# Attention, dense layer and experts in one kernel: expert layer over token groups of 256, 1024, 1024 in place of 768, 768, 768

## The chip, the cores and the metric

One core of one Trainium2 chip runs one program. The metric is device time in microseconds (us): the median of the runs of one kernel on the core.

## The reference, cut to what is computed

```
p_packed = softmax(p k^T / 8) v ; a = softmax(q p_packed^T / 8) p_packed     # 4 batches, 8 heads, 576 positions, 32 packed
x = silu(a w_in) w_out                                                       # 2304 tokens, 512 -> 2048 -> 512
P = exp(x w_gate - max); 8 times: rows to 1, columns to 1, times 2304 / 8    # 2304 x 8 experts
out = sum over e of P[:, e] * (relu(x w1[e]) w2[e])                          # w1 512 x 1024, w2 1024 x 512
```

All 2304 tokens go through all 8 experts.

## The kernel before, in words

Each product of the dense layer and of the experts is made of three TensorE products: an operand is split into a high part (ScalarE copies it to fp32r, line 113) and a low part (VectorE subtracts, line 114), and high·high, high·low and low·high are added in PSUM. This pair, `split`, makes every "form" below. Every stationary operand is 128 x 128; the streamed one has as many columns as the matmul is wide.

**Front and dense layer.** The attention of the four batches and the first quarter (c = 0) of the dense layer's hidden columns run in an order that a planner (`Plan`, lines 150 to 205) writes out: tasks have an engine, a cost, a priority (the tables `P_A1` to `P_C1`) and buffers that they take and give; `LOADS` is the order of the loads on the DMA queue. The weights of the dense layer come as 64-bit words, which `conv` turns to fp32. When the attention is over, `close_att` frees its memory, and the conversions of the second quarter (c = 1) begin. Then c = 1, 2, 3 follow, each of 8 half batches: 4 tiles of `gemm1` (line 522, 6 matmuls of 288 columns, then silu and a split) and 4 tiles of `gemm2` (line 556, 12 matmuls of 288 columns, of the half batch before), and once per batch a product `u` (line 215). After each tile `pump()` lets one piece of background work be placed. At the end of c = 3 the background is `pre_forms`: the forms of x and of the first expert weights. Outside the planner's part the framework orders the instructions of each engine itself, by their place in the text and by when it expects buffers and operands.

**Experts.** The 2304 tokens are three groups of 768, in two halves of `BLK` = 384. A step is an expert and one half of its hidden columns: 16 steps in a group, 48 in all (`NS`). Up (`up`, line 849) is a Strassen-Winograd scheme: 7 products of 12 matmuls, each of 384 columns. Down of group 0 (`down`, line 892) is plain: 6 tiles of 12 matmuls of 512 columns. Down of groups 1 and 2 (`down7`, line 985) is again 7 products of 12 matmuls of 384 columns: `h_forms` makes 7 forms of the hidden values, 768 wide, from 4 differences; products are added to seven sums `M`, by a seeded bank and ScalarE's copies (lines 981, 993) or on VectorE (line 995).

The 7 forms of w1 and of w2 that each step needs are made in group 0 from the loaded weights (`w1_forms`, `w2_split`), stored in DRAM (`put`, line 650, 512 KB a form), and loaded (`get`) by groups 1 and 2. Group 0 has two buffers `T` for w2's forms and a ring of 16 buffers of 512 KB (`unit`) for the others. The column and row scaling of P (`sinkhorn`, lines 1005 to 1070) is a chain of small VectorE instructions that runs beside the first steps of group 0.

```
        for c in range(2):
            x = xf[g, p]
            for l, r in ((0, 0), (0, 1), (1, 0)):
                pe.matmul(ps, w[:, l, c, 128 * i:128 * i + 128], x[:, r, c],
...
        for f in range(4):
            w, h = w2t[s][f], hT[s, half, f]
            for l, r in ((0, 0), (0, 1), (1, 0)):
                pe.matmul(ps, h[:, l, 128 * tt:128 * tt + 128], w[:, r], start=(n == 0), stop=(n == 11))
```

Of the kernel before, what the change touches and what calls it, by code (L numbers as in the profile page):

```python
# [23 lines left out]
BLK = 384  # L24
FH = 512
EPS = 1e-9
CP = 6
# [3 lines left out]
P_A1 = [33.24, 7.01, 10.96, 13.54]  # L31
P_A2 = [49.27, 35.77, 44.16, 62.94]
P_U = [38.81, 12.22, 18.2, 4.05]
P_G1 = [23.84, 10.29, 0.56, 25.68]
P_G2 = [31.18, 0, 4.18, 31.19]
P_CI, P_CO, P_C1 = 0, 0.24, 33.0

LOADS = "k0 i2 i3 i1 i0 v0 q0 k1 q1 v1 o0 g k2 v2 o1 o3 q3 o2 v3 q2 k3"
# [35 lines left out]
def fused_kernel(  # L74
# [29 lines left out]
    a2b_p, a2b_st = pool("a2b", 1, side="right")  # L104
# [23 lines left out]
    class Plan:  # L128
# [13 lines left out]
        def order(self):  # L142
# [6 lines left out]
            while left:  # L149
# [46 lines left out]
                for c, k in t["give"]:  # L196
# [6 lines left out]
                 "a1T": 2, "ppm": 2, "ct": 4, "one": 1, "y": 4, "cr": 4})  # L203
# [49 lines left out]
    def plan_attention(b, early, late):  # L253
# [42 lines left out]
        for g in both:  # L296
# [8 lines left out]
            add(f"t{g}", "PE", 0.75, tr, [f"e{g}"], take=[("p", 2 - g)], give=[("a1", 1)])  # L305
# [22 lines left out]
        add("v", "PE", 1.3, pp, ["c0", "c1", ("v", b, 0), ("v", b, 1)], take=[("p", 1)],  # L328
# [287 lines left out]
    GRP = [(3, 4), (5, 0), (1, 2)]  # L616
    steps = [(g, e, fh) for g in range(3) for e in range(NE) for fh in range(2)]
    NS = len(steps)
    ORD = [1, 2, 6, 7, 5, 3, 4]
# [3 lines left out]
    st = {}  # L623
    raw1, raw2, wf, w2t, xf = {}, {}, {}, {}, {}
    x2d = tc.dram_tile([DM // 128, 128, NT], F32, name="x2d")

    def load_w1(s, kh):
        if s >= 2 * NE:
            return
# [6 lines left out]
    def load_w2(s, j):  # L636
        if s >= 2 * NE:
            return
        _, e, fh = steps[s]
        t = st["r2"].tile([128, 2, DM], F32, tag="r2", name=f"r2_{s}{j}")  # L640
# [4 lines left out]

    w1d, w2d = {}, {}

    def put(d, s, p, t):
        d[s, p] = tc.dram_tile([128, 2, 2, 256], F32, name=f"{'w1' if d is w1d else 'w2'}d{s}_{p}")
        nc.sync.dma_start(d[s, p], t.bitcast(F32))  # L650

    def get(d, s, p):
        t = unit([128, 2, 2, 256], F32R, f"{'w1' if d is w1d else 'w2'}l{s}_{p}")
        nc.sync.dma_start(t.bitcast(F32), d[s % (2 * NE), p])
        return t

    def w1_loads(s):
        for p in ORD:
            if s < NS:
                wf[s, p] = get(w1d, s, p)  # L660
            yield
            yield

    def w2_loads(s):
        for p in DORD:
            w2f[s, p] = get(w2d, s, p)
            yield
            yield

    def w1_forms(s, tmp):  # L670

        if s >= NS:
            return
        k1, k2 = raw1[s, 0], raw1[s, 1]
        a11, a21 = k1[:, :, 0:256], k1[:, :, 256:512]
        a12, a22 = k2[:, :, 0:256], k2[:, :, 256:512]

        def form(p, src):
            t = unit([128, 2, 2, 256], F32R, f"wf{s}_{p}")
            split(t[:, 0], t[:, 1], src)  # L680
            wf[s, p] = t
            put(w1d, s, p, t)

        form(1, a11)
        yield
        form(2, a12)
        yield
        s1, s2, s3, s4 = tmp(s, 1), None, None, None
        dve.tensor_tensor(s1, a21, a22, op=ALU.add)
        s2 = tmp(s, 2)  # L690
        dve.tensor_tensor(s2, s1, a11, op=ALU.subtract)
        form(6, s2)
        yield
        s3 = tmp(s, 3)
        dve.tensor_tensor(s3, a11, a21, op=ALU.subtract)
        load_w1(s + 1, 0)
# [4 lines left out]
        s4 = tmp(s, 4)  # L701
        dve.tensor_tensor(s4, a12, s2, op=ALU.subtract)
        form(3, s4)
        yield
        form(4, a22)
        load_w1(s + 1, 1)
        yield

    def w2_split(s):
        if s >= NS:  # L710
            return
        w2t[s] = []
        for j in range(2):
            for f in range(2):
                t = unit([128, 2, DM], F32R, f"w2t{s}{j}{f}")
                split(t[:, 0], t[:, 1], raw2[s, j][:, f])
                w2t[s].append(t)
                for p in ((1,) if j == 0 else (2, 4)):
                    if f == 0:
                        w2d[s, p] = tc.dram_tile([128, 2, 2, 256], F32, name=f"w2d{s}_{p}")  # L720
                    c = 256 if p == 4 else 0
                    nc.sync.dma_start(w2d[s, p][:, :, f], t[:, :, c:c + 256].bitcast(F32))
                yield

        k1, k2 = raw2[s, 0], raw2[s, 1]
        a11, a21 = k1[:, :, 0:256], k1[:, :, 256:512]
        a12, a22 = k2[:, :, 0:256], k2[:, :, 256:512]

        def form(p, src):
            t = st["T"].tile([128, 2, 2, 256], F32R, tag="T", name=f"T{s}_{p}")  # L730
            split(t[:, 0], t[:, 1], src)
            put(w2d, s, p, t)

        s1 = s_tmp(s, 11)
        dve.tensor_tensor(s1, a21, a22, op=ALU.add)
        s2 = s_tmp(s, 12)
        dve.tensor_tensor(s2, s1, a11, op=ALU.subtract)
        form(6, s2)
        yield
        s3 = s_tmp(s, 13)  # L740
        dve.tensor_tensor(s3, a11, a21, op=ALU.subtract)
        load_w2(s + 1, 0)
# [4 lines left out]
        s4 = s_tmp(s, 14)  # L747
        dve.tensor_tensor(s4, a12, s2, op=ALU.subtract)
# [322 lines left out]
    def nopump():  # L1071
        pass
# [213 lines left out]
```

## Time and profile before

| | us |
|---|---|
| median of 3 runs (1844.19 to 1844.93) | 1844.29 |
| the profiled execution, whole | 1845.25 |
| its span, first to last instruction | 1843.5 |
| TensorE busy in the span | 1812.1 |
| VectorE busy | 1317.4 |
| ScalarE busy | 924.9 |

The profile is one execution. PE is TensorE's matmuls, PEld its weight loads, DVE VectorE, ACT ScalarE, SP the queue that issues DMAs. Times in rows are us from the span's start, "x16" counts instructions, "out<-in" are tiles by their names in the program. Matmuls overlap in the array, so that the duration of one is longer than the distance to the next; the distance is read from rows that span many. VectorE's and ScalarE's durations overlap too, by about 0.1 us.

### The profile page before, as it was taken

The numbers are of one execution on the slowest core, as the hardware profiler recorded it, in microseconds if no ns is written. First come the engines' busy times: TensorE is split into PE (matmuls) and PEld (weight loads), VectorE is DVE, ScalarE is ACT, GpSimd is POOL, SyncE is SP. The second block draws the span as 40 slices with busy tenths as digits, with TensorE's granted clock in tenths as the row PEclk, the third lists the DMA queues.
The fourth block names the chain that finished last, engine by engine and source line by source line (L and its number), as shares of the span: only waits on it lengthen the run. The fifth ranks groups of instructions, "written<-read, shape, count | busy, mean of one in ns | idle before, by whom it ended". The sixth has DMA issues, their size and how long they took to land.

```text
span 1843.5 us, 29407 instructions
## 1 busy us (share of the span) xinstructions
PE 1812.1 (98%) x11127; PEld 1716.8 (93%) x11127; DVE 1317.4 (71%) x2228; ACT 924.9 (50%) x1816; POOL 1.0 (0%) x8
## 2 busy tenths in 40 slices
PE   6999999999999999999999999999999999999998
PEld 3898999998899989899999999999999999999998
DVE  6877644769987878787556667576786767666676
ACT  4876443545454545444254554454555445444544
POOL 0000000000000000000000000000000000000000
PEclk8999999999999999999999999999999999999999
DMA  9332100288898888888887878888888887888872
GB/s 336 117 92 93 58 13 1 75 285 319 304 338 297 312 296 306 302 308 296 302 263 250 261 258 261 261 245 266 259 275 287 250 266 256 263 247 261 262 251 95
DMA packets 169116, 437.18 MB, mean 237 GB/s; under 512 B 15360, under 2 KB 63632, under 8 KB 168976
## 3 DMA queue, kind: packets, MB, share of 16 engines
q1 hardware_dynamic: 168976, 435.31, 71.4%
q8 instruction: 88, 1.44, 0.3%
q14 instruction: 52, 0.43, 0.1%
HBM read 309.87 MB, written 125.38 MB: 236 GB/s over the span
## 4 chain that ended last, share of the span: by engine, by line
PE 95%; DMA 2%; DVE 1%; ACT 1%; issue 0%; SPq 0%; DVEq 0%; ACTq 0%
PE d L985 25%; PE X L849 22%; PE m L892 14%; PE Z L849 11%; PE g L556 10%; PE Y L849 5%; PE g L522 5%; PE u L215 1%; DMA k<-in_kT_dram 1%; DMA v<-in_v_dram 1%; PE s L215 1%; DMA rawin<-in_moe_w_in_dram 0%; PE lg L1011 0%; PE pp L323 0%; PE tp L302 0%
## 5 line engine op out<-in xcount | busy, mean ns | idle before, releaser
L985 PE MATMUL d<-hi,w2l 128*128 128x384 f32 x1792 | 495.0, 336 | 0.0
L114 DVE TENSOR_TENSOR lo<-hb,hi 128x768 fp32r<-128x768 f32 x224 | 214.2, 957 | 267.7 <-PE d L985 209.3
L985 PEld LDWEIGHTS d<-hi,w2l 128*128 128x128 f32 x1792 | 327.0, 188 | 6.8 <-ACT d L981 6.8
L985 PE MATMUL d<-lo,w2l 128*128 128x384 f32 x896 | 299.4, 334 | 0.0
L849 PE MATMUL X<-xf,w1l 128*128 128x384 f32 x1536 | 286.8, 334 | 0.0
L892 PE MATMUL m<-w2t,h 128*128 128x512 f32 x1152 | 280.4, 393 | 0.0
L849 PEld LDWEIGHTS X<-xf,w1l 128*128 128x128 f32 x1536 | 268.1, 188 | 0.1
L892 PEld LDWEIGHTS m<-w2t,h 128*128 128x128 f32 x1152 | 214.2, 188 | 41.9 <-DVE cp L860 0.3
L993 ACT COPY M<-d 128x384 f32<-128x384 f32 x232 | 111.6, 481 | 220.0 <-PE d L985 219.8
L113 ACT CAST hi<-hb 128x768 fp32r<-128x768 f32 x224 | 184.1, 836 | 57.7 <-DVE hb L946 30.9
L856 ACT COPY cp<-X 128x384 f32<-128x384 f32 x224 | 107.5, 480 | 209.8 <-PE X L849 209.8
L556 PE MATMUL g<-gT,woh 128*128 128x288 f32 x1024 | 206.4, 297 | 0.0
L556 PEld LDWEIGHTS g<-gT,woh 128*128 128x128 f32 x1024 | 163.8, 188 | 10.6 <-DVE gT L530 5.9
L985 PEld LDWEIGHTS d<-lo,w2l 128*128 128x128 f32 x896 | 168.2, 188 | 0.0
L556 PE MATMUL g<-gT,wol 128*128 128x288 f32 x512 | 150.7, 294 | 0.0
L849 PE MATMUL X<-xf,wf 128*128 128x384 f32 x768 | 146.7, 338 | 1.7 <-ACT cp L856 1.7
L849 PEld LDWEIGHTS X<-xf,wf 128*128 128x128 f32 x768 | 135.9, 188 | 8.3 <-ACT cp L856 2.9
L849 PE MATMUL Z<-xf,w1l 128*128 128x384 f32 x768 | 143.4, 334 | 0.0
L849 PEld LDWEIGHTS Z<-xf,w1l 128*128 128x128 f32 x768 | 134.0, 188 | 0.0
L995 DVE TENSOR_TENSOR M<-d,M 128x384 f32<-128x384 f32 x204 | 112.7, 552 | 10.9 <-PE d L985 10.6
L522 PE MATMUL g<-a2h,U 128*128 128x288 f32 x512 | 110.9, 301 | 5.8 <-ACT U L500 3.9
L981 ACT COPY d<-M 128x384 f32<-128x384 f32 x216 | 104.5, 484 | 18.1 <-DVE hb L822 14.8
(170 smaller groups left out, 2344.9 us busy)
## 6 DMA issues: line engine op xcount, KB each, us to landing
w1l<-w1d SPq DMA_DIRECT2D x224, 512.0 KB, 4.7
w2l<-w2d SPq DMA_DIRECT2D x224, 512.0 KB, 4.4
w1d<-wf SPq DMA_DIRECT2D x112, 512.0 KB, 5.3
r<-in_moe_w_dram SPq DMA_DIRECT2D x64, 512.0 KB, 5.9
w2d<-T SPq DMA_DIRECT2D x64, 512.0 KB, 4.3
w2d<-w2t SPq DMA_DIRECT2D x96, 256.0 KB, 3.6
rawin<-in_moe_w_in_dram SPq DMA_DIRECT2D x16, 512.0 KB, 4.8
rawout<-in_moe_w_out_dram SPq DMA_DIRECT2D x16, 512.0 KB, 4.7
```

The costliest lines, as they stand in the source:

```text
L113: act.copy(out=hi, in_=raw)
L114: eng.tensor_tensor(out=lo, in0=raw, in1=hi.bitcast(F32), op=ALU.subtract)
L215: pe.matmul(outs[i][32 * k:32 * k + 32, :n], lhsT[r, 32 * k:32 * k + 32], rhs(k)[r, cols], start=True, stop=True)
L522: pe.matmul(ps[:, :HS], lhs, rhs, start=(n == 0), stop=(n == 5))
L556: pe.matmul(ps[:, :HS], lhs, rhs, start=(n == 0), stop=(n == 3 * nf - 1))
L849: pe.matmul(ps, w[:, l, c, 128 * i:128 * i + 128], x[:, r, c], start=(n == 0 and p in ((1, 7) if g else (1, 2, 7))), stop=(n == 5), skip_g ...
L856: act.copy(out=t, in_=ps)
L892: pe.matmul(ps, h[:, l, 128 * tt:128 * tt + 128], w[:, r], start=(n == 0), stop=(n == 11))
L981: act.copy(out=ps, in_=m)
L985: pe.matmul(ps, w[:, l, c, 128 * d:128 * d + 128], r[:, c], start=(n == 0 and not seed), stop=(n == 5), skip_group_check=seed)
L993: act.copy(out=m, in_=ps)
L995: dve.tensor_tensor(m, ps, m, op=ALU.add)
```

## The change

- The expert groups become 256, 1024 and 1024 tokens. Group 0 (the first and the last 128 tokens) is plain on both sides: `up0` (4 blocks of 12 matmuls of 256 columns) and `down0` (2 tiles of 12 of 512). Groups 1 and 2 keep the 7 products, now 512 columns wide; hidden values, their forms and the sums `M` grow from 384 or 768 to 512 or 1024 elements.
- The forms of w1 for 12 of the 16 steps (`FRONT`) are made and stored by `pre_w1` during c = 1, 2, 3 of the dense layer, through two buffers `po`: 18, 28 and 38 forms are placed there in the text. Those of steps 5, 7, 9, 11 are made in group 0 (`w1_rest`). Group 0 itself needs only a plain split of w1 and w2 per step (`w1_split`, `w2_split`). w2's forms are made in group 1 (`w2_forms`), used there and stored; group 2 loads them.
- `pre0` splits x of group 0 and the weights of step 0 at the end of c = 3. The forms of x for group 1 are made in steps 10 to 14 of group 0, those for group 2 in group 1, stored and loaded in its last step.
- P is needed from expert 3 on (`LATE`); the results of experts 0 to 2 wait in six buffers.
- The planner's priorities, the order of the loads and two of its costs are others, and the conversions of c = 1 have three buffers in place of four.

```diff
-BLK = 384
+LG = 384
+NB = 512
+FRONT = [0, 1, 2, 3, 4, 6, 8, 10, 12, 13, 14, 15]
+RATE = {1: 18 / 64, 2: 28 / 64, 3: 38 / 44}
+LATE = 3
+AHEAD = 3
...
-LOADS = "k0 i2 i3 i1 i0 v0 q0 k1 q1 v1 o0 g k2 v2 o1 o3 q3 o2 v3 q2 k3"
+LOADS = "o2 i0 k0 i1 i3 v0 k3 i2 q0 o3 k1 g v3 k2 v1 q2 o1 v2 o0 q1 q3"
...
-                 "a1T": 2, "ppm": 2, "ct": 4, "one": 1, "y": 4, "cr": 4})
+                 "a1T": 2, "ppm": 2, "ct": 4, "one": 1, "y": 4, "cr": 3})
...
-            add(f"t{g}", "PE", 0.75, tr, [f"e{g}"], take=[("p", 2 - g)], give=[("a1", 1)])
+            add(f"t{g}", "PE", 0.9, tr, [f"e{g}"], take=[("p", 2 - g)], give=[("a1", 1)])
...
-        add("v", "PE", 1.3, pp, ["c0", "c1", ("v", b, 0), ("v", b, 1)], take=[("p", 1)],
+        add("v", "PE", 2.5, pp, ["c0", "c1", ("v", b, 0), ("v", b, 1)], take=[("p", 1)],
...
-    GRP = [(3, 4), (5, 0), (1, 2)]
+    TOK, TIL = {1: 1152, 2: 128}, {1: 9, 2: 1}
+    T0 = ((1, 8 * 128, 17), (0, 0, 0))
...
+    def pre_w1(todo, then):
+            def form(p, x):
+                t = st["po"].tile([128, 2, 2, 256], F32R, tag="po", name=f"po{s}_{p}")
+                split(t[:, 0], t[:, 1], x)
+                put(w1d, s, p, t)
...
+    def halves(name, s, j, raw):
+        h = unit([128, 2, 512], F32R, f"{name}h{s}{j}")
+        l = unit([128, 2, 512], F32R, f"{name}l{s}{j}")
+        split(h, l, raw)
...
+    def up0(s, j):
+        for i in range(2):
+            n = 0
+            f = slice(128 * (2 * j + i), 128 * (2 * j + i) + 128)
+            for k in range(4):
+                wh, wl = w1t[s][k // 2]
+                for w, x in ((wh, xs[0]), (wh, xs[1]), (wl, xs[0])):
+                    pe.matmul(ps[:, i], w[:, k % 2, f], x[:, k], start=(n == 0), stop=(n == 11))
...
+    def down0(s, tt):
+        for f in range(4):
+            wh, wl = w2t[s][f // 2]
+            h = h0[s, f // 2]
+            for l, w in ((0, wh), (0, wl), (1, wh)):
+                pe.matmul(ps, h[:, l, f % 2, 128 * tt:128 * tt + 128], w[:, f % 2],
+                          start=(fh == 0 and n == 0), stop=(fh == 1 and n == 11))
...
-    for name, n in (("cp", CP), ("T", 2), ("r2", 2), ("S", 3), ("h", 12), ("acc", 6)):
+    for name, n in (("xf", 7), ("cp", 5), ("xr", 2), ("pb", 2)):
...
-        for name, n, side in (("pb", 2, "left"), ("hb", 6, "left"), ("M", 8, "left"), ("hi", 5, "left"),
-                              ("lo", 4, "left")):
+    for name, n in (("hb", 6), ("hi", 3), ("lo", 3)):
...
+                if swap:
+                    nc.sync.dma_start(x_tile(2, p).bitcast(F32), xfd[p])
+                q = 7 * s + n + AHEAD
+                if q < 7 * NS:
+                    wf[q // 7, ORD[q % 7]] = get(w1d, q // 7, ORD[q % 7])
...
+            q = 7 * (s - 1) + n + AHEAD
+            if G0 <= q // 7 < 2 * G0:
+                next(forms)
+            elif 2 * G0 <= q // 7 < NS:
+                w2f[q // 7, DORD[q % 7]] = get(w2d, q // 7, DORD[q % 7])
```

## Rows read from the trace of the kernel before

**Rows 1.** The page: busy us, share of the span and count of each engine.
```profile
PE 1812.1 (98%) x11127; PEld 1716.8 (93%) x11127; DVE 1317.4 (71%) x2228; ACT 924.9 (50%) x1816; POOL 1.0 (0%) x8
```

**Rows 2.** Stretches: length; PE, PEld, DVE, ACT, POOL busy; granted clock, DMA share, GB/s.
```profile
0.00:20.00 20.00, 9.44 (x127) 5.21 (x127) 10.59 (x21) 9.52 (x20) 0.99 (x8) 1.00 0.95 339
20.00:40.00 20.00, 14.77 (x219) 6.79 (x219) 15.35 (x22) 8.61 (x18) 0.00 (x0) 0.77 0.99 317
40.00:60.00 20.00, 16.59 (x228) 11.64 (x229) 18.31 (x33) 17.89 (x41) 0.00 (x0) 0.89 0.83 279
...
100.00:141.30 41.30, 37.44 (x291) 36.37 (x289) 32.47 (x63) 33.18 (x76) 0.00 (x0) 0.99 0.34 103
141.30:222.60 81.30, 81.28 (x620) 77.27 (x621) 55.70 (x119) 44.69 (x103) 0.00 (x0) 0.97 0.25 80
222.60:303.60 81.00, 81.00 (x640) 76.98 (x639) 40.80 (x87) 33.99 (x82) 0.00 (x0) 1.00 0.04 13
303.60:386.90 83.30, 83.30 (x651) 80.13 (x652) 50.47 (x106) 35.73 (x88) 0.00 (x0) 1.00 0.29 105
386.90:480.00 93.10, 89.86 (x484) 77.36 (x485) 84.53 (x198) 46.15 (x90) 0.00 (x0) 1.00 0.86 304
480.00:500.00 20.00, 20.00 (x101) 17.96 (x100) 19.59 (x36) 9.91 (x19) 0.00 (x0) 1.00 0.84 301
480.00:896.40 416.40, 416.40 (x2073) 374.97 (x2072) 338.37 (x566) 195.10 (x376) 0.00 (x0) 1.00 0.87 308
896.40:1834.20 937.80, 937.80 (x5370) 929.86 (x5370) 632.10 (x965) 469.84 (x868) 0.00 (x0) 1.00 0.80 254
```

**Rows 3.** The chain of waits: start us, us, what; dense layer, group 0, group 2.
```profile
283.23 6.39 PE g L556 x48
...
638.49 2.76 PE m L892 x12
...
857.45 2.76 PE m L892 x12
...
1445.43 2.27 PE d L985 x12
...
1797.11 2.27 PE d L985 x12
```

**Rows 4.** Groups by line and form: instruction, tiles and count, then busy us, mean ns.
```profile
L404 DVE TENSOR_TENSOR a2l<-a2f,a2h 128x1152 fp32r<-128x1152 f32 x4 | 5.4, 1355 | 0.6 <-ACT a2h L399 0.6
L114 DVE TENSOR_TENSOR lo<-hb,hi 128x768 fp32r<-128x768 f32 x224 | 214.2, 957 | 267.7 <-PE d L985 209.3 <-ACT d L981 53.0 <-ACT hi L113 5.4
L114 DVE TENSOR_TENSOR wf<-S,wf 128x512 fp32r<-128x512 f32 x60 | 40.1, 685 | 0.3 <-ACT wf L113 0.2
L113 ACT CAST wf<-S 128x512 fp32r<-128x512 f32 x60 | 36.0, 621 | 17.7 <-DVE S L702 11.3 <-DVE S L691 3.8 <-DVE S L695 1.9
L914 DVE SCALAR_TENSOR_TENSOR acc<-m,P,acc 128x512 f32<-128x512 f32 x84 | 62.9, 749 | 34.2 <-PE m L892 34.1
...
L1048 DVE TENSOR_REDUCE csum<-P 128x8 f32<-128x144 f32 x8 | 3.3, 418 | 0.0
```

**Rows 5.** Group 0's stores of w2's forms, by tile.
```profile
DMA to landing us min/median/max: 2.6/4.3/8.5
```

**Rows 6.** DMA issues: KB each, median us to landing; 330 to 365 us, then 600 to 900.
```profile
w1d<-wf SPq DMA_DIRECT2D x3, 512.0 KB, 2.8
...
w1d<-wf SPq DMA_DIRECT2D x56, 512.0 KB, 5.4
```

**Rows 7.** By tile: dense weights of c = 2, 3: ns min/median/max, first and last start us.
```profile
L445 DVE CUSTOM_DVE_ANT_0 win<-rawin,ctin x8: 681/683/687, 151.8 to 216.9; 128x1024 uint16<-128x1024 uint16 x8
```

**Rows 8.** The chain of waits in the front: start us, us, what.
```profile
5.34 10.31 DMA v<-in_v_dram
...
26.93 9.11 DMA k<-in_kT_dram
...
135.34 3.85 DMA rawin<-in_moe_w_in_dram
```

More of the change, by code (lines that the diff above doesn't have):

```diff
@@ new lines, in pre_w1, with w1_split @@
+            s4 = sums(s, 4, ALU.subtract, a12, s2)
+            load_w1(nxt, 0)
+            load_w1(nxt, 1)
+            form(7, s3)
+            yield
+            form(5, s1)
+            yield
+            form(3, s4)
+            yield
+    w1t, w2t = {}, {}
+    def halves(name, s, j, raw):
+        h = unit([128, 2, 512], F32R, f"{name}h{s}{j}")
+        l = unit([128, 2, 512], F32R, f"{name}l{s}{j}")
+        split(h, l, raw)
+        return h, l
+    def w1_split(s):
+        w1t[s] = []
+        for j in range(2):
+            w1t[s].append(halves("w1", s, j, raw1[s, j]))
+            if s in FRONT and s + 1 < G0:
+                load_w1(s + 1, j)
+            yield
@@ new lines, in fused_kernel, with chain @@
+    open_("acc", 2 * LATE)
+    st["m"], s_ = pool("pm", 2, space=PSUM, side="left", reuse_waits="tile"); ctx.enter_context(s_)
+    def chain(*gens):
+        for g in gens:
+            yield from g
+    rest = iter(())
+    xg = x_forms(1, x_keep)
+    for s in range(G0 + 1):
+        wa = w1_split(s + 1) if s + 1 < G0 else iter(())
+        wb = w2_split(s) if 0 < s < G0 else iter(())
+        for slot in range(4):
+            if slot % 2 == 0:
+                if s < G0:
+                    up0(s, slot // 2)
+            elif s > 0:
+                if s == 2 * LATE + 2 and slot == 1:
+                    for _ in sk:
+                        pass
+                    load_pb(1, 0)
+                down0(s - 1, slot // 2)
+            if s == G0:
+                continue
+            next(wa if slot < 2 else wb, None)
+            if slot == 1 and s + 1 < G0 and s + 1 not in FRONT:
+                rest = w1_rest(s + 1)
+            if slot >= 1:
+                next(rest, None)
+            if s >= 1 and slot % 2:
+                next(sk, None)
+            if s >= 10 and slot:
+                next(xg, None)
+        for _ in rest:
+            pass
+        if s == G0 - 2:
+            for _ in xg:
+                pass
+        if s == G0 - 2:
+            for p in ORD[:AHEAD]:
+                wf[G0, p] = get(w1d, G0, p)
@@ L1205, in fused_kernel @@
+    for name in ("acc", "r2", "gh", "po"):
+        closers[name].close()
+    for name, n in (("hb", 6), ("hi", 3), ("lo", 3)):
+        open_(name, n, keep=True)
+    load_w2(G0, 0, "r1")
+    load_w2(G0, 1, "r1")
+    forms = chain(*(w2_forms(s) for s in range(G0, 2 * G0)))
+    xg = x_forms(2, x_store)
+    for s in range(G0, NS + 1):
+        swap = s + 1 < NS and steps[s + 1][0] != steps[s][0]
         hform = h_forms(s - 1) if s > G0 else iter(())
```

576 lines of the change are left out of this document (256 added, 320 removed).

## The prediction, made before the changed kernel ran

> **What bounds the kernel now.** I read the page's busy line first: TensorE is busy for 1812.1 of 1843.5 us [rows 1]. Then the stretches, to see where it is not [rows 2]: the front (to 141.3 us) leaves 23.1 us of TensorE idle (10.6, 5.2, 3.4 and 3.9 in the four rows that have any), the first 93.1 us of the expert layer leave 3.2 us, and the rest is full: 416.40 of 416.40 and 937.80 of 937.80 us. So from c = 1 on the time is the number of matmuls by the distance between them; another engine counts only where it makes TensorE wait. The chain of waits gives the distances, as periods that span many matmuls [rows 3]. A `gemm2` run of 48 matmuls of 288 columns takes 6.39 us: 133.1 ns each. In group 2, 12 steps of 168 matmuls of 384 columns lie between 1445.43 and 1797.11 us: 29.307 us a step, 174.4 ns each. In group 0, 7 steps lie between 638.49 and 857.45 us: 31.28 us a step; less 84 at 174.4 ns, 16.63 us are left for 72 of 512 columns: 230.9 ns each. From 288 to 384 columns that is 0.430 ns a column, from 384 to 512 it is 0.441.
>
> The terms below are differences against the span of that execution (1843.5 us; 1845.25 us whole, 0.96 above the median), and are put on the median of 1844.29 us. About 0.2% (3.7 us) is what a measurement here can tell from no change.
>
> **1. The matmuls: -16.7 us.** Before: 16 x 31.28 + 32 x 29.307 = 500.5 + 937.8 = 1438.3 us. After, groups 1 and 2 have the same 168 matmuls a step at 512 columns: 32 x 168 x 230.9 ns = 1241.3 us. Group 0 has 48 of 256 and 24 of 512 columns a step. No row has 256 columns; going on from 288 along 0.430 ns a column gives 119.3 ns, so 5.73 + 5.54 = 11.27 us a step, 180.3 us in 16. Sum 1421.6 us. There are 0.8% fewer columns and 1344 fewer matmuls of 7872. For 256 columns 133.1 ns (the 288 row) is the upper bound, if the weight loads set a floor there; that takes 10.6 us of the gain. Below, in proportion to columns, it is 118.3 ns. I take the line, since three widths lie on it.
>
> The Trainium skill's TensorE: Matmul & The Clock Gate, section Back-to-back issue gap, has columns / 2.4 GHz + 2.5 ns for one matmul after another. By it 384 columns would be 162.5 ns and 512 would be 215.8; the rows say 174.4 and 230.9, so the trace does not agree. The sum by the page would be 1340.6 to 1326.8, -13.8 us in place of -16.7, and the forecast 1838.
>
> **2. The dense layer: +3 us (0 to +8.5).** 84 forms of w1 come in, each a ScalarE cast of 0.621 and a VectorE subtraction of 0.685 us, with 48 sums of 0.685 us [rows 4]: VectorE +90.4 us. Out go the old forms at its end (14 of 0.55 us on halves of x with 8 differences, on the line of those rows, about 12 us, and 11 x 0.685), and in come 8 splits of 128 columns and 8 halves of 512 KB for step 0, about 8 us. The rows of c = 1, 2, 3 have 55.7 + 40.8 + 50.5 = 147 us of VectorE in 245.6; after, about 226, 92%. What hides it is VectorE's idle time. Rows on both sides of this: 19.59 of 20 us with TensorE at 20.00, and 84.53 of 93.1 (91%) with 3.24 us lost [rows 2]. At the second row's rate 245.6 us would lose 8.5. The first is steady work like this, the second a start with the sinkhorn beside it, so I take a third. ScalarE rises from 114 to about 160 of 245.6 us and is not near. Each engine takes its instructions in order: a cast that waits for one of the two `po` buffers holds up the silu behind it, and TensorE then waits for the PSUM bank that this silu frees. This is the rival below.
>
> The forms are placed late in the text (38 of 84 in c = 3, where 38 x 0.524 MB and 5.4 pairs of loads of 1.05 MB make 25.6 MB, over 44 of 64 pumps, 56 us: 457 GB/s, more than any row's 339). But work isn't kept to its place: the weights of c = 3, whose conversions stand in the text of c = 2 (from 222.6 us), were all done by 216.9 [rows 7]. So I expect the forms to spread from 141 us on, 65 MB with all loads in 245.6 us, 265 GB/s.
>
> **3. Group 0: +4 us (0 to +16).** The cover gets thin here, since TensorE's step shrinks from 31.28 to 11.27 us. VectorE per step: 4 halves of 1024 elements at 1.22 us (between 957 ns at 768 and 1355 at 1152 [rows 4]), 2 of 0.69 for the hidden values, about 0.7 for the sums (749 ns): 7.0 us. Steps 4, 6, 8, 10 add `w1_rest`: 4 sums and 4 splits, 5.5 us; steps 10 to 14 add 3.2 us for x's forms; the sinkhorn's 8 rounds have 8 small instructions of at most 418 ns, at most 27 us over steps 1 to 7. In all 112 + 22 + 15 + 27 = 176 us of 180.3 as the upper end, by durations that overlap. Each weight has buffers for two steps, so a step can lend to the next. Stalls at the rate of the like stretch before (3.24 in 93.1 us) are 6.3 us in place of 3.2, +3; I add 1 for the DMA, which has 58 MB in 180 us, 322 GB/s against 304 before, and 349 in steps 4 to 11 (2.1 MB of loads a step and 3.7 MB of stores in every second one). The upper end is each step's own surplus: 5.1, 5.1, 1.2 and 4.4 us in steps 4, 6, 8, 10, 15.8 us.
>
> **4. Groups 1 and 2: +2 us (0 to +10).** Step 38.79 us. VectorE in group 1: 11 of 1024 elements at 1.22, 30 of 512 at 0.69 (hidden values 8, additions 4 and 7, w2's forms 11), 1 for x: 35.1 us, 91% by durations; less about 0.08 us of overlap on each of 42, 31.7 us, 82%. Group 0 before had 338.37 of 416.40 (81%) and lost nothing [rows 2]. In group 2 it is 68%. The step before group 2 loads 7 x 1.05 MB of x beside 7.3 MB of weights, 379 GB/s: at most 4.5 us late at the fullest row's 339. With three buffers for `hi` and `lo` a late form shows sooner than with 5 and 4.
>
> **5. The front: -2 us (-10 to +9).** The work is the same; the order is not seen in this trace. Before, the chain waits 10.31 us for v and 9.11 for k, and 3.85 for raw weights that ScalarE's queue met too early [rows 8]. The bytes up to the end of v0 are the same in the new order (o2 i0 k0 i1 i3 v0 against k0 i2 i3 i1 i0 v0), the second k comes before a q fills the buffers, and the last loads are q1 and q3, for which half of the attention is already done, in place of k3. Against it: k0 is two loads (3 us at 339 GB/s) later, and c = 1 has three conversion buffers for four. The gain ends well inside the 23.1 us idle; the loss end is one more wait like the 9.11 row. I take little, on the side of the loads.
>
> **6. The tail: +0.5 us.** Last additions and stores are a third wider, with nothing beside them.
>
> Sum: -16.7 + 3 + 4 + 2 - 2 + 0.5 = -9.2; 1844.3 - 9.2 = **1835 us**.
>
> **Rivals.**
> - The front takes the 9 us wait for k away and more: 1844.3 - 16.7 - 10 + 9.5 = 1827 or less. For: VectorE has 14 us idle in the first 40 [rows 2]. Against: VectorE is already at 18.31 of 20 us from 40 on. Chance 0.20.
> - The gain is eaten: weight loads floor the 256 columns (+10.6), or stalls of 3 to 5 near half of their upper ends: 1841 to 1848. For: nothing here is narrower than 288. Against: 288 columns still lie on the line of 384 and 512. Chance 0.10.
> - Slower: VectorE sets the pace wherever the forms now lie. Upper ends of 2, 3 and 4 together, 8.5 + 15.8 + 10 = 34.3 us: 1844.3 - 16.7 - 2 + 0.5 + 34.3 = 1860. It decides from 18.2 us of stalls on. For: 91% with losses in the row from 386.9 us. Against: 98% without any in the row from 480. Chance 0.13.
> - Slower: the two `po` buffers pace the 84 forms. A buffer turns in 0.62 + 0.69 + the store + about 0.3 us of hand-overs; at a store of 5.4 us (the median at 304 GB/s) that is 3.5 us a form, 294 us in 245.6: +48, 1881. At 2.8 us (the median when little else ran) it is 2.2 us a form, 185 us [rows 6]. It decides from 4.2 us on; group 0's two `T` buffers had 4.3 in the middle [rows 5]. Against: with two stores out at a time and 265 GB/s the queue is shorter, and TensorE stood still for none of those. Chance 0.07.
> - The forecast, 1828 to 1840: 0.50.
>
> **How the numbers follow.** Faster 0.20 + 0.50 = 0.70, within 0.2% 0.10, slower 0.20. The range goes from 1822 (front at -10, stalls at half) to 1856 (most of the VectorE rival); outside lie some 0.06 below and 0.12 above.
>
> **What would show it.** Right: steps of 38.8 us in groups 1 and 2 and of 11.3 in group 0, 256-column matmuls at 119 ns, c = 1 beginning within a few us of 141 and taking 81.3 us a quarter, TensorE idle under 10 us behind it. Wrong: ScalarE waiting on the stores of `po` with silus behind it; TensorE waiting on VectorE in steps 4 to 10 of group 0; w1's forms unfinished at the end of c = 3; a front longer than 146 us.

## The result and the profile after

The changed kernel takes 1820.82 us (median of 4 runs, 1817.46 to 1822.23) against 1844.61 us of the kernel before beside it (1844.19 to 1845.57): a ratio of 0.9866, interval 0.9851 to 0.9882. The gain of 23.8 us is two and a half times the 9.2 forecast, and 1820.82 lies 1.2 us below the range of 1822 to 1856. The profiled execution took 1820.67 us, its span is 1818.7.

The busy line of the page, which answers to [rows 1]:

```profile
PE 1779.1 (98%) x9783; PEld 1513.0 (83%) x9783; DVE 1396.1 (77%) x1994; ACT 1004.6 (55%) x1674; POOL 1.0 (0%) x8
```

Stretches of the kernel after, with the columns of [rows 2]: the quarters c = 1, 2, 3, group 0 in two parts, groups 1 and 2, and then four slices of 20 us out of c = 1 and 2.

```profile
138.60:222.70 84.10, 80.09 (x593) 74.39 (x594) 71.79 (x147) 51.76 (x117) 0.00 (x0) 0.94 0.67 232
222.70:309.40 86.70, 84.58 (x642) 78.30 (x641) 70.46 (x141) 50.58 (x115) 0.00 (x0) 0.98 0.70 253
309.40:396.90 87.50, 87.50 (x676) 83.59 (x678) 63.52 (x125) 48.93 (x109) 0.00 (x0) 1.00 0.76 275
396.90:490.00 93.10, 93.04 (x626) 81.64 (x627) 85.20 (x162) 54.05 (x75) 0.00 (x0) 1.00 0.78 258
490.00:592.30 102.30, 98.91 (x604) 89.48 (x603) 64.53 (x76) 44.39 (x56) 0.00 (x0) 0.97 0.86 286
592.30:1204.00 611.70, 611.08 (x2694) 505.16 (x2694) 510.60 (x664) 356.55 (x553) 0.00 (x0) 1.00 0.74 248
...
140.00:160.00 20.00, 20.00 (x148) 19.00 (x148) 17.49 (x36) 13.64 (x34) 0.00 (x0) 0.92 0.61 212
...
180.00:200.00 20.00, 15.99 (x105) 13.50 (x104) 17.41 (x38) 11.11 (x26) 0.00 (x0) 0.83 0.64 215
...
220.00:240.00 20.00, 17.88 (x134) 15.68 (x132) 16.63 (x37) 11.88 (x27) 0.00 (x0) 0.97 0.81 280
240.00:260.00 20.00, 20.00 (x148) 19.39 (x142) 17.00 (x33) 11.94 (x27) 0.00 (x0) 0.95 0.64 237
```

The chain of waits of the kernel after, with the columns of [rows 3]: first the dense layer, then group 0, the start of group 1, and the same product 11 steps apart in group 2.

```profile
181.01 7.38 DMA rawin<-in_moe_w_in_dram
188.47 0.67 ACT ctin L438
...
190.64 0.61 ACT po L118
191.25 0.32 ACT graw L531
191.62 2.73 PE u L220 x16
...
440.69 2.75 PE d L883 x12
443.43 2.87 PE u L864 x24
...
559.17 14.00 DMA r<-in_moe_w_dram
...
592.28 2.72 PE X L1011 x12
...
1339.20 2.72 PE d L968 x12
...
1758.08 2.72 PE d L968 x12
```

Set against the boundaries of the kernel before (c = 1 from 141.3, the logits after c = 3 from 386.8, the first expert product at 392.1, group 0's last at 900.9, which is its end at 903.2 less 2.3 us for 13 matmuls of group 1 that ran ahead of it, the end at 1843.5), each term has a measured size:

| step | forecast | measured | from |
|---|---|---|---|
| 1 matmuls | -16.7 | -39.9 | 38.080 us a step in groups 1 and 2 ((1758.08 - 1339.20) / 11), 11.24 in group 0 (twice 2.87 and 2.75) |
| 2 dense layer | +3 | +12.8 | 258.3 us for 245.5 |
| 3 group 0 | +4 | +2.0 | 10.3 us over its matmuls for 8.3 |
| 4, 6 groups 1, 2, tail | +2.5 | +3.1 | 7.8 us over their matmuls for 4.7 |
| 5 front | -2 | -2.8 | c = 1 from 138.5 for 141.3 |
| sum | -9.2 | -24.8 | the spans differ by 24.8 |

So two terms were wrong, with opposite signs: step 1 by 23.2 us, step 2 by 9.8. They hide each other in part: with step 2 as forecast the time would have been about 1811 us. The experiments are on these two.

### The profile page after: what moved, and what is told of

Same layout as the page of the kernel before. It is cut to its first block, busy times and chain, and to the rows that moved or that the text cites. A ratio compares the mean times of both kernels' runs of the same rounds, so it can differ in the third digit from the quotient of the medians.

```text
span 1818.7 us, 26101 instructions
## 1 busy us (share of the span) xinstructions
PE 1779.1 (98%) x9783; PEld 1513.0 (83%) x9783; DVE 1396.1 (77%) x1994; ACT 1004.6 (55%) x1674; POOL 1.0 (0%) x8
## 4 chain that ended last, share of the span: by engine, by line
PE 82%; DMA 8%; DVE 6%; ACT 2%; issue 1%; SPq 0%; DVEq 0%; ACTq 0%
PE d L968 31%; PE X L1011 18%; PE Z L1011 9%; PE g L561 8%; PE Y L1011 5%; PE g L527 4%; DMA r<-in_moe_w_dram 4%; PE u L864 2%; PE d L883 2%; DMA rawin<-in_moe_w_in_dram 1%; DMA rawout<-in_moe_w_out_dram 1%; PE u L220 1%; DMA w1d<-po 1%; DMA k<-in_kT_dram 1%; DVE S L671 1%
## 5 line engine op out<-in xcount | busy, mean ns | idle before, releaser
L1011 PE MATMUL X<-xf,w1l 128*128 128x512 f32 x1536 | 368.8, 389 | 0.0
L1011 PEld LDWEIGHTS X<-xf,w1l 128*128 128x128 f32 x1536 | 288.3, 188 | 59.9
L119 DVE TENSOR_TENSOR lo<-hb,hi 128x1024 fp32r<-128x1024 f32 x224 | 273.4, 1221 | 51.6 <-ACT hi L118 50.6
L118 ACT CAST hi<-hb 128x1024 fp32r<-128x1024 f32 x224 | 236.0, 1054 | 107.8 <-PE d L968 99.8
L968 PE MATMUL d<-hi,w2f 128*128 128x512 f32 x896 | 294.6, 389 | 0.6 <-ACT d L964 0.6
L968 PE MATMUL d<-hi,w2l 128*128 128x512 f32 x896 | 293.1, 389 | 0.0
L968 PEld LDWEIGHTS d<-hi,w2f 128*128 128x128 f32 x896 | 168.2, 188 | 36.6 <-ACT d L964 1.7
L968 PEld LDWEIGHTS d<-hi,w2l 128*128 128x128 f32 x896 | 168.1, 188 | 35.2 <-ACT d L964 0.4
L1011 PE MATMUL Z<-xf,w1l 128*128 128x512 f32 x768 | 184.5, 389 | 0.0
L968 PE MATMUL d<-lo,w2f 128*128 128x512 f32 x448 | 174.3, 389 | 0.0
L968 PE MATMUL d<-lo,w2l 128*128 128x512 f32 x448 | 174.3, 389 | 0.0
L968 PEld LDWEIGHTS d<-lo,w2l 128*128 128x128 f32 x448 | 84.1, 188 | 17.5
```

The source lines that it names most:

```text
L118: act.copy(out=hi, in_=raw)
L119: eng.tensor_tensor(out=lo, in0=raw, in1=hi.bitcast(F32), op=ALU.subtract)
L968: pe.matmul(ps, w[:, l, c, 128 * d:128 * d + 128], r[:, c], start=(n == 0 and not seed), stop=(n == 5), skip_group_check=seed)
```

## Experiments

"Quarters" are the times of c = 1, 2, 3, from the first `gemm1` matmul of one to that of the next. Before they are 77.6, 81.3 and 86.6 us, after 84.1, 86.7 and 87.5. Each run has its own median of before beside it; between sets of runs those medians go from 1844.6 to 1846.7. Times without an interval are of one execution.

### What a matmul of 512 columns costs

**The kernel before, with the six down tiles of group 0 in a row** at the end of a step, in place of one behind each up product:

```diff
-            elif n > 0 and s > 0:
-                down(s - 1, n - 1)
-                pump_sk()
-                bg()
+            elif n == 6 and s > 0:
+                for d in range(6):
+                    down(s - 1, d)
+                    pump_sk()
+                    bg()
```

> The kernel before with one change: in the steps of group 0 the six plain down tiles follow each other after all seven up products, 72 matmuls of 512 columns in a row in place of six runs of 12 between products of 384 columns. Nothing is left out. Theory (mixed widths): matmuls of one width follow each other at columns / 2.4 GHz + 13.3 ns (384: 173.3, 512: 226.7 ns), and some ten matmuls after each change of width are a few ns slower; then the 72 take 16.36 us in each step, as the one such run in the trace before does, the step falls from 31.28 to 30.95 us, and the time by 5 us, to 1839. Rival (plain down): a tile with hidden values as its stationary operand costs 230.9 ns a matmul wherever it stands; then the step stays at 31.28 us and the time at 1844.

The chain of waits of this kernel in group 0:

```profile
629.07 16.36 PE m L892 x72
645.43 2.10 PE X L849 x12
647.54 2.08 PE Y L849 x12
...
876.64 5.48 PE m L892 x24
```

TensorE's largest wait between 380 and 480 us (line waited, releaser, us, times, longest):

```profile
PE cs L1051 <- DVE csum L1048: 10.0, 3, 5.7
```

72 matmuls of 512 columns in a row take 16.36 us, 227.2 ns each, and the step is (876.64 - 629.07) / 8 = 30.946 us in place of 31.28. The forecast of the whole time failed: 1856.87 us, ratio 1.0059 [1.0042, 1.0075]. The steps gained 0.33 us each, but the first ones lost more, since without a down tile to run in between TensorE waited 10.0 us for the column sums of the sinkhorn, and the granted clock from 387 to 480 us was 0.89, for 1.00 before [rows 2]. The price is settled all the same: 230.9 ns is the price of a 512-column matmul that stands in twelves between twelves of 384, and 227 that of one among its like. The trace of the kernel before had the same thing in its last step of group 0, where nothing of 384 columns stands in between, in a row of the chain that I had not used; with the last step's neighbours:

```profile
881.79 2.76 PE m L892 x12
884.55 2.10 PE X L849 x12
...
886.83 16.36 PE m L892 x72
903.19 1.93 PE Y L849 x11
905.12 2.08 PE X L849 x12
```

Twelve take 2.76 us after a change of width and 2.72 after their like (the chain after); of 384 columns twelve take 2.10 after a change and 2.08 without. Groups 1 and 2 of the changed kernel have one width throughout.

### Which part of the forms costs the dense layer 13 us

**No forms in the dense layer** (those of step 0 alone are made, and groups 1 and 2 load these for all the steps of `FRONT`):

```diff
+        k = 0 if d is w1d and s % G0 in FRONT else s % G0
-        nc.sync.dma_start(t.bitcast(F32), d[s % G0, p])
+        nc.sync.dma_start(t.bitcast(F32), d[k, p])
-    pre = pre_w1(FRONT, 0)
+    pre = pre_w1([0], 0)
```

> The kernel after without the background forms of w1: only those of step 0 are made and stored; groups 1 and 2 load step 0's forms for the other eleven steps, so that the loads there stay the same. Left out: 77 casts, 77 subtractions, 44 sums, 77 stores and 22 loads of the dense layer. If the forms are the cause of the longer dense layer, c = 1 to c = 3 return from 258.3 us to 245.5, as before, and the time to about 1808. If the cause is the three buffers or the other order, they stay above 252.

1810.13 us; quarters 77.5, 81.3 and 86.6, which are the kernel before's. So the forms are the whole loss, and the third conversion buffer or the other priorities have no part in it by themselves. **A fourth conversion buffer**, as before (`pool("cv", 3` to `4`), says the same from the other side:

> The kernel after with four buffers in place of three for the raw dense weights and their conversions (the planner's order of the front stays as it is). Nothing is left out. Theory (late weights): c = 1 and c = 2 are 6 us longer each than before because conversions of dense weights stand in ScalarE's queue ahead of silus and wait for loads that land late beside the stores of w1's forms. If the three buffers are what makes these loads start late, c = 1 to c = 3 (258.3 us from the first gemm1 of c = 1 to the logits) fall by 6 us or more, to 252, and the time to 1814. Rival (traffic): the loads are late because of the forms' stores and loads beside them; then a fourth buffer gives under 2 us.

1818.10 us, ratio 0.9850 [0.9835, 0.9864]; quarters 79.0, 87.7, 90.3, 257.0 in all.

Four runs then took one part of the forms away each. **The forms made, but only step 0's stored** (`if s == 0: put(w1d, s, p, t)`, and the same `k` for the loads):

> The kernel after with all forms of w1 made in the dense layer, but only those of step 0 stored (groups 1 and 2 load step 0's forms for the other eleven). Left out: 77 stores of 512 KB. VectorE and ScalarE do the same work. Theory (late weights): the DMA traffic is what makes the weights late and the two po buffers slow, so c = 1 to c = 3 fall to within 3 us of 245.5. Rival (VectorE or ScalarE full): they stay above 254, since both engines have as much to do as in the kernel after.

**Raw weights loaded and stored, no arithmetic** (in `form`, for all steps but 0, a store of the raw tile in place of the split, and no sums):

> The kernel after with the stores and loads of w1's forms in the dense layer, but without their making: for eleven of the twelve steps the raw weights are stored in the form's place. Left out: 77 casts, 77 subtractions and 44 sums. Theory (engines): with the stores gone but the forms made, c = 1 to c = 3 still took 256.8 us, so the casts, subtractions and sums in the queues of ScalarE and VectorE are the cause, and here they fall to 245.5 to 248 us. Rival (traffic): stores and loads delay the dense weights by themselves; then they stay above 252.

**All forms made and stored, from step 0's raw weights** (22 loads left out):

```diff
-            load_w1(nxt, 0)
-            load_w1(nxt, 1)
+            if nxt == then:
+                load_w1(nxt, 0)
+                load_w1(nxt, 1)
+            else:
+                raw1[nxt, 0], raw1[nxt, 1] = raw1[s, 0], raw1[s, 1]
```

> The kernel after with all forms made and stored, but from step 0's raw weights each time: 22 loads of 512 KB of the dense layer are left out (the forms are then those of step 0 under eleven other names). Theory (VectorE full): casts, subtractions, sums and stores are as many as before, so c = 1 to c = 3 stay above 255. Rival (waits in order for these loads): they fall to 250 or less.

**The 48 sums on GpSimd** (`nc.gpsimd.tensor_tensor` in `sums`, for `pre_w1` alone):

> The kernel after with the 48 sums of the forms in the dense layer made by GpSimd in place of VectorE. Nothing is left out. Theory (VectorE full): in the run without stores VectorE was 18.8 of 20 us busy from 140 to 300 us, so 29 us less of VectorE's work there give back half or more of the 12.8 us: c = 1 to c = 3 at 252 or less, the time at 1814. Rival (waits in order): the time is lost where a cast or a sum waits in its queue for a load and holds up what is behind; then c = 1 to c = 3 stay within 3 us of 258.

| | quarters | sum | time |
|---|---|---|---|
| no stores | 81.3, 88.9, 86.6 | 256.8 | 1819.67 |
| loads and stores alone | 78.0, 88.7, 86.6 | 253.3 | 1815.54 |
| no loads | 77.9, 83.9, 86.6 | 248.4 | 1811.61 |
| sums on GpSimd | 90.3, 86.7, 91.8 | 268.8 | 1833.81, ratio 0.9939 [0.9924, 0.9954] |

The stretches of c = 1 and 2 without the loads:

```profile
137.50:215.50 78.00, 76.82 (x590) 71.25 (x591) 71.90 (x150) 53.27 (x120) 0.00 (x0) 1.00 0.58 210
215.50:299.40 83.90, 83.24 (x642) 77.70 (x641) 72.31 (x146) 51.36 (x115) 0.00 (x0) 1.00 0.57 218
```

VectorE is busy here for 71.90 of 78.00 and 72.31 of 83.90 us, 89% of both together, more than the 83% of the changed kernel's two (142.25 of 170.8): the same work in less time, and TensorE stands idle for 1.8 us. So VectorE's share is not what costs. Part of this run's small loss is luck, though. The granted clock of its c = 1 is 1.00, while the kernel before has 0.97 there [rows 2], after a wait of 3.9 us before its first `gemm1`. That is some 2.4 us of the 245.5 (0.03 of 81.3), so that from an equal start the loss without loads is about 5 us and not 2.9.

Traffic alone, with VectorE at the level of before, costs 7.8 us, in a single wait of 4.5 us and the lower clock behind it (0.96 in c = 2). Without the stores 11.3 of the 12.8 us stay. What the three runs take away (9.9, 5.0 and 1.5 us) is more than the whole, so the parts don't add, and no one of them accounts for the loss alone.

The sums on GpSimd met neither expectation. On GpSimd a sum takes 1331 to 1535 ns, and VectorE's own subtractions get longer beside it, from 684 to 799 ns in the mean:

```profile
L119 DVE TENSOR_TENSOR po<-S,po 128x512 fp32r<-128x512 f32 x64 | 51.1, 799 | 27.6 <-ACT po L118 27.5
...
L671 POOL TENSOR_TENSOR S<-r,S 128x512 f32<-128x512 f32 x12 | 18.4, 1535 | 18.2 <-DVE po L119 18.2
...
L671 POOL TENSOR_TENSOR S<-S,r 128x512 f32<-128x512 f32 x12 | 16.0, 1331 | 10.9 <-PE g L561 6.1 <-DVE po L119 4.2
```

### Where TensorE waits, and for what

TensorE's waits of the changed kernel from 138 to 397 us, and the largest of ScalarE's (the columns as above):

```profile
PE u L220 <- ACT graw L531: 6.1, 3, 4.0
PE g L527 <- ACT U L505: 3.1, 1, 3.1
...
ACT po L118 <- DMA w1d<-po: 42.9, 31, 3.6
ACT ctin L438 <- DMA rawin<-in_moe_w_in_dram: 9.2, 4, 4.5
ACT ctout L438 <- DMA rawout<-in_moe_w_out_dram: 3.9, 2, 2.8
```

TensorE waits only three times for a silu, always at the product `u` that takes a PSUM bank from `gemm1`; the wait at the first `gemm1` of c = 1 is in the kernel before too, with 3.9 us. The longest, 4.0 us, stands in the chain after: a load of dense weights (`rawin`, 7.38 us to landing) ends at 188.4, ScalarE converts it, casts two forms, and only then runs the silu for which `u` waits at 191.6. Without the forms the same `u` takes 1.02 us at 189.62:

```profile
186.43 3.19 PE g L527 x24
189.62 1.02 PE u L220 x16
190.64 6.54 PE g L561 x48
```

ScalarE's own timeline shows what stood ahead of each of the three silus (start us, us, instruction, in brackets the idle time before it and what ended it):

```profile
188.47 0.66 ACT L438 ACTIVATE ctin<-rawin 128x512 f32<-128x512 f32 x1 [4.45 <-DMA rawin<-in_moe_w_in_dram]
...
234.78 0.66 ACT L438 ACTIVATE ctout<-rawout 128x512 f32<-128x512 f32 x1 [2.78 <-DMA rawout<-in_moe_w_out_dram]
...
237.38 0.67 ACT L439 ACTIVATE rawout<-rawout 128x512 uint32<-128x512 uint32 x1 [1.09 <-DMA rawout<-in_moe_w_out_dram]
```

TensorE's waits end at 191.62, 236.35 and 238.72 us, each with the silu behind one of these. So in this trace it is three times a conversion of a dense weight whose load had not landed, and not once a cast that waited for a form buffer, although ScalarE waits longer for those in all.

The 6.1 us of waiting cost more than 6.1. A slice of 20 us at the full granted clock holds 160 of these matmuls. Of the four slices shown first, the last three hold 105, 134 and 148, which is 93 fewer or 11.6 us. The last has no idle time at all and still lacks 12 matmuls, at a granted clock of 0.95; the slice of 0.83 has the 4.0 us wait in it. The first, with 148 at 0.92, stands behind the wait before the first `gemm1`, and there the kernel before lost more:

```profile
140.00:160.00 20.00, 18.68 (x128) 17.68 (x129) 13.40 (x27) 11.57 (x27) 0.00 (x0) 0.83 0.25 78
```

So about half of the 12.8 us is waiting, and most of the rest is matmuls at the lower of the two clock levels (1.2 for 2.4 GHz) after a wait: granted clocks of 0.83, 0.97 and 0.95 over 20 us each are 5.0 us less at the full clock.

What ScalarE stands for can be one of three: a raw weight (no such wait of ScalarE shows in the changed kernel), a form buffer whose store has not landed, a late dense weight. Eight runs tried to take one away. **Sums first, loads one form earlier** (`pre_w1` makes all four sums ahead of form 6 and issues the next loads behind it), and **two more raw buffers, loads a step ahead**:

```diff
-RATE = {1: 18 / 64, 2: 28 / 64, 3: 38 / 44}
+RATE = {1: 18 / 64, 2: 28 / 64, 3: 38 / 40}
...
-        for s, nxt in zip(todo, todo[1:] + [then]):
+        for n, (s, nxt) in enumerate(zip(todo, todo[1:] + [then])):
+            raw = raw1[s, 0], raw1[s, 1]
+            load_w1(nxt, 0, "r1" if n % 2 else "rr")
+            load_w1(nxt, 1, "r1" if n % 2 else "rr")
```

> The kernel after with the four sums of each step of w1 made first and the loads of the next step's raw weights issued after the third form in place of the fourth: one form (some 2.5 us) more between a load and its first use. Work and traffic are the same. Theory (loads): without these loads c = 1 to c = 3 took 248.4 us at the same busy time of VectorE and ScalarE, so what costs is that a cast or a sum stands in its queue before its raw weights have landed; a lead of one form more gives back 3 us or more, to 255 or less, the time to 1817. Rival (traffic): the loads cost by sharing the DMA engines with the dense weights; then nothing changes, 258 us.

> The kernel after with two more buffers for raw weights of w1 in the dense layer (the steps take turns), so that the loads of a step are issued a whole step, seven forms, before they are used; the forms end four tiles earlier. Work and traffic are the same. Theory (loads): c = 1 to c = 3 fall to 248 to 251 us, as without the loads, and the time to 1811 to 1814, faster than the kernel after by 7 to 10 us. Rival (traffic): within 3 us of 258, the time at 1818 to 1821.

**Three form buffers** (`po` 2 to 3, `cp` 5 to 4, for its memory), **the dense weights' conversions twice as early in the text** (a second `cvn.step()` in each pump of c = 1 and 2), and **both**:

> A third buffer for the forms of w1 that the dense layer makes (memory taken from the copies of w_1: four buffers for five). If ScalarE's queue stands at casts that wait for a buffer whose store has not landed (46 us of its waits in c = 1 to 3 of the changed kernel) and holds up the silus behind it, these waits fall to under 15 us, the dense quarters c = 1 to 3 take at most 252 us in place of 258.3, and the time is at most 1815 us. If the stores' landing only shows where ScalarE happens to stand and something else is late, the quarters stay within 3 us of 258 and the time within 1817 to 1822.

> The conversions of the dense layer's own weights for the next quarter stand twice as early in the text of c = 1 and 2. If TensorE waits in c = 1 and 2 because these weights, whose loads share the DMA queue with the forms' loads and stores, are converted late, the quarters c = 1 to 3 take at most 254 us in place of 258.3 and the time is at most 1817 us. If the weights are in time and the loss is the silus' place in the queues, the quarters stay within 3 us of 258; if the conversions in a row push silus back, they take 261 or more.

> Three form buffers (alone 253.1 us in the quarters c = 1 to 3 and 1813.2 us) and the dense weights' conversions twice as early in the text (alone 1815.8 us as a median, with one profiled execution at 260.4 us in the quarters). If ScalarE's silus are held up by two things, casts that wait for a form buffer and conversions that wait for late dense weights, the two edits add: quarters of 248 to 251 us, 1808 to 1811 us. If both only shift the same waits, the time is 1812 to 1816.

**Other DMA queues.** SP's queue, which issues every transfer in order, stands 110.6 us in c = 1 and 2 at stores of forms that VectorE has not made yet. The dense weights' loads, and in another run the stores, went to GpSimd's queue (`nc.gpsimd.dma_start`); a third joined the first with three form buffers:

> The loads of the dense layer's own weights for c = 1 to 3 go through GpSimd's DMA queue in place of SP's, where in c = 1 and 2 of the changed kernel the queue stands 111 us at stores of forms that VectorE has not made. If the dense weights come late because their loads stand behind these stores in one queue in order, the waits of SP's queue at those loads go, the dense quarters c = 1 to 3 take at most 251 us in place of 258.3, and the time is at most 1814 us. If the weights come late because the DMA engines are shared with 50 MB of other traffic, or are in time anyway, the quarters stay within 3 us of 258.

> The stores of the forms made in the dense layer go through GpSimd's DMA queue; all loads keep SP's. If it is the stores that hold up the loads behind them in SP's queue, the quarters c = 1 to 3 take at most 252 us and the time is at most 1815 us; the loads of raw expert weights still stand in SP's queue and wait for a free buffer, so that this may help less than moving the dense weights' loads. If the loss is not made by the queue's order, within 3 us of 258.

> Both: the dense weights' loads on GpSimd's queue, and a third buffer for the forms (which alone gave 253.1 us in the quarters and 1813 us). If queue order and the two buffers are separate costs, the quarters take 246 to 250 us and the time is 1805 to 1811; if they are one and the same, the time is that of the better one alone.

| | quarters | sum | time | ratio |
|---|---|---|---|---|
| changed kernel | 84.1, 86.7, 87.5 | 258.3 | 1820.82 | 0.9866 [0.9851, 0.9882] |
| sums first | 83.4, 86.8, 88.9 | 259.1 | 1818.87 | 0.9853 [0.9836, 0.9869] |
| two more raw buffers | 81.5, 84.1, 89.8 | 255.4 | 1813.88 | 0.9824 [0.9809, 0.9839] |
| three form buffers | 80.7, 85.1, 87.3 | 253.1 | 1813.21 | 0.9822 [0.9806, 0.9838] |
| conversions earlier | 80.8, 86.2, 93.3 | 260.4 | 1815.75 | 0.9843 [0.9818, 0.9867] |
| both of these | 83.4, 86.0, 90.5 | 259.9 | 1816.97 | 0.9842 [0.9825, 0.9858] |
| dense loads on GpSimd's queue | 86.3, 90.4, 89.1 | 265.8 | 1829.90 | 0.9912 [0.9897, 0.9926] |
| with three form buffers | 85.6, 92.9, 87.1 | 265.6 | 1833.16 | 0.9928 [0.9911, 0.9945] |
| form stores on GpSimd's queue | 84.8, 96.2, 107.3 | 288.3 | 1857.38 | 1.0064 [1.0049, 1.0079] |

Sums first changed nothing in the quarters: its theory, the lead of the loads, failed. Two edits gain clearly, by some 7 us each: a third form buffer, and two more raw buffers. Both beat the kernel before and the changed one. Their expectations were met in the time (at most 1815, and 1811 to 1814) and not in the quarters (253.1 for at most 252, and 255.4 for 248 to 251), and that of the third buffer not in the mechanism: ScalarE's waits for the stores should have fallen under 15 us, and are 41.0, hardly less than 42.9. What both change is the length of TensorE's waits and the clock. The waits for silus are 4.6 and 5.3 us in all for 6.1, but the longest is 2.0 us in both for 4.0, and the granted clock of c = 1 and 2 is 0.98 and 1.00 for 0.94 and 0.98, some 5 us of full clock. First three form buffers, then two more raw buffers:

```profile
139.30:220.00 80.70, 78.29 (x591) 71.77 (x592) 73.73 (x154) 53.91 (x122) 0.00 (x0) 0.98 0.71 261
220.00:305.10 85.10, 82.73 (x642) 77.57 (x641) 74.44 (x150) 54.21 (x120) 0.00 (x0) 1.00 0.83 303
...
140.60:222.10 81.50, 78.11 (x592) 72.81 (x592) 71.31 (x147) 52.55 (x119) 0.00 (x0) 0.98 0.69 239
222.10:306.20 84.10, 83.50 (x642) 77.74 (x641) 69.95 (x142) 50.00 (x113) 0.00 (x0) 1.00 0.74 265
```

Not all of either gain lies in the quarters: they give 5.2 and 2.9 us, and group 0 gives 4.0 and 4.4. The late raw weight near its end (14.00 us at 559.17 in the chain after) takes 12.80 and 11.95 us there, TensorE's wait behind it is 1.5 and 0.7 us in place of 3.4, and the granted clock stays at 1.00, where the changed kernel has 0.97 in the second part of group 0. The two were not run together.

The conversions did not add to the third buffer: they took its gain in the quarters away, and about half of it in the time (0.9842 for 0.9822 and 0.9866, with intervals that overlap). Alone, they met their expectation in the time (1815.75 for at most 1817) and not in the quarters (260.4 for at most 254). ScalarE's waits for dense weights fall from 16.1 to 7.9 us, but those for form buffers rise from 42.9 to 68.3, and TensorE's for silus from 6.1 to 7.5. The profiled execution of that run was the slowest of its four (1824.05; the others 1814.77 to 1815.92), so that its quarters are worse than its median.

GpSimd's queue is no way out. It issues through an instruction of 531 ns on GpSimd itself:

```profile
L661 POOL DMA_DIRECT2D w1d<-po x84: 531/531/788, 99.6 to 402.6; - x84
```

That is the tile's stores in the kernel with the stores on that queue (ns min/median/max, first and last start). Its waits from 138 to 440 us:

```profile
ACT po L118 <- DMA w1d<-po: 92.2, 47, 5.3
...
PE u L220 <- ACT graw L531: 25.9, 9, 5.2
```

A store takes 531 ns to issue for 320 on SP and 3.8 us to landing in the median for 3.3. With a buffer's turn longer by these 0.7 us ScalarE waits 92.2 us for buffers, TensorE 25.9 us for silus, and the quarters take 30 us more. That the loads on GpSimd's queue made the layer longer too means that the test can't say what SP's order costs: the queue that took its place has a price of its own.

**The dense layer in the order of the text** (c = 1 to 3 under a schedule by hand, so that the framework draws nothing forward):

> The kernel after with the instructions of TensorE, VectorE and ScalarE in c = 1 to c = 3 kept in the order of the text, so that the framework can't draw forms forward: 18, 28 and 38 in c = 1, 2, 3. Nothing is left out. If the loss comes from forms and conversions drawn forward into c = 1 and c = 2 (VectorE's stretches there 17 of 20 us against 12 before), these two return to within 2 us of 77.6 and 81.3 us, and c = 3 pays for it: 38 forms of 1.09 us of VectorE by rows, with 36 us of its own, are 77 of 86.6 us, and their 19.9 MB of stores and 5.7 MB of loads are 457 GB/s over 56 us, so c = 3 is longer by 10 us or more, and the sum no better than 258.

1880.39 us, ratio 1.0194 [1.0177, 1.0211], quarters 83.1, 103.6, 135.9. TensorE waits 40.4 us for silus here, ScalarE 71.7 us for stores and 43.7 for sums. c = 3 paid as expected, but c = 1 and 2 did not return to 77.6 and 81.3, so drawing forms forward does not by itself explain the loss there. The place in the text is bad (38 forms in c = 3), and the framework's order is better, in which the forms run from 98.5 to 366.3 us. This run fixes the order of all three engines and not of the forms alone, so it does not show which move of the framework's helps.

## Why the prediction was wrong, point by point

**Step 1 failed, and it is the term that sets the sign of the miss.** As put there: "less 84 at 174.4 ns, 16.63 us are left for 72 of 512 columns: 230.9 ns each". The subtraction was right, but what it priced is a step of mixed widths, and the changed groups have one width. Measured are 226.67 ns (38.080 us / 168): 32 x 168 x 4.23 ns = 22.7 us, nearly all of the 23.2. The step gave 256 columns a range on both sides and 512 none, so that no part of the forecast's range stood for this miss. The 256 columns themselves came at 119.6 ns (24 in 2.87 us) for 119.3. Per column the trace agrees with the Trainium skill's TensorE: Matmul & The Clock Gate, section Back-to-back issue gap: from 256 to 512 columns (226.7 - 119.6) / 256 = 0.418 ns, which is 1 / 2.4 GHz, where I had taken 0.430 to 0.441. The constant beside it is 13.3 ns in this trace (226.67 - 213.33) and not the 2.5 that the page gives for an isolated gap.

**Step 2 failed in its size and its engine.** As put there: "At the second row's rate 245.6 us would lose 8.5", "so I take a third", "ScalarE rises from 114 to about 160 of 245.6 us and is not near". The loss is 12.8 us, over the upper bound. The bound was worked out from VectorE's busy share, and the run without loads had a higher share and a smaller loss. The sentence behind it, that an instruction that waits holds up the silu in ScalarE's queue, was the mechanism; I used it for one rival alone (two `po` buffers pace the forms), priced it as a rate of forms, and thought only of casts that wait for `po`. The rate was no bound: the forms ended at 366 us. In the changed kernel the silus stood behind conversions that waited 4.45, 2.78 and 1.09 us for dense weights, and for late dense weights the sum had no term. What was missing besides is that three silus late by 0.8 to 4.0 us are enough, because the granted clock is down after them. VectorE rose to 205.8 us, not the 226 forecast, and 11.6 us of the difference are 9 of the 84 forms and 8 of the 48 sums that were done in the front ((9 + 8) x 0.685).

**Steps 3 to 6 came near their numbers, 3 and 5 by luck.** The front began c = 1 2.8 us earlier (forecast 2), but not by less waiting, which was the reason given. TensorE's wait for k grew (the kernel before, then the changed one, to 142 and 140 us):

```profile
PE s L215 <- DMA k<-in_kT_dram: 6.6, 3, 5.5
...
PE s L220 <- DMA k<-in_kT_dram: 11.0, 3, 8.3
```

All its idle time there is 23.2 us for 23.1. What is shorter is its busy time, 115.3 for 118.3 us, with granted clocks of 0.91 and 0.83 from 20 to 60 us where [rows 2] has 0.77 and 0.89. Group 0 lost 2.0 us (4), and not to VectorE's amount of work, for which step 3 had 3 of the 4: at 85.20 of 93.1 us VectorE cost TensorE 0.06 us there, where [rows 2] had 3.24 at 84.53; the loss came later, in one late load and the lower clock behind it (0.97 in the second part). Groups 1 and 2 show no wait of TensorE on VectorE: 510.60 of 611.70 us is 83%, as forecast (82), with 0.62 us idle.

**The rivals.** VectorE as the pace fell, the front's 10 us did not come, and the 256 columns had no floor by weight loads. The nearest in number, 1827 or less, would have been right for a wrong reason.

**What is shown and what stays open.** Shown: the forms are the whole loss of the dense layer (it is gone without them); VectorE's busy share, the conversion buffers and the lead of the loads by one form are not its cause; it consists of a few late silus and the lower clock behind them; in the changed kernel these silus stand behind dense weights that landed late. The sums of ScalarE's waits do not tell the loss: they are 42.9 us for stores and 16.1 for dense weights after, 44.3 and 16.3 without the loads, where the loss is far smaller. What matters is which silu stands behind a wait. Only argued: that the turn of the form buffers matters in itself. One more buffer gains and a longer turn goes with 30 us more, but both runs change the order as well. Open: why the dense weights come late (the order of SP's queue, the traffic or the free buffers), and why the clock fell so much less behind the waits in the two runs that gain. Every edit gives the framework another order, and the arrangements that differ only in buffers or in places in the text lie between 253 and 260 us, so that a difference of 3 us between two of them says little of its cause.

## What to carry to other kernels

Take the price of a matmul from a run of its own width, and put a bound on both sides of the one price that multiplies most of the work: 4 ns on 5376 matmuls were 23 us here. When background work goes under a bound engine, ask first what stands behind it in the queue of the engine that frees that engine's buffers; its busy share says little (ScalarE was at 59% of the dense layer here), and a spare buffer is worth a try: a third form buffer gave 7.6 us.

## What the runs showed of the hardware that was not expected

- A change of width costs TensorE some 0.02 to 0.04 us in the first dozen of matmuls after it: 2.76 for 2.72 us (512 columns), 2.10 for 2.08 (384).
- The distance of these fp32r matmuls, each with a weight load of its own, is columns / 2.4 GHz and 13 ns, from 256 (119.6) over 288 (133) and 384 (173.3) to 512 columns (226.7). The 174.4 ns of group 2 before are a mean in which one product of 12 in each step took 2.27 us in place of 2.08.
- A GpSimd sum of two 128 x 512 operands (1331 to 1535 ns) lengthens VectorE's subtraction beside it from 684 to 799 ns in the mean.
- A DMA issued by GpSimd takes 531 ns of that engine, and its store lands 0.5 us later in the median than one issued by SP.
